# Two of block 10's four gelu groups moved from tile to tile by 48 KB transfers instead of through DRAM

## The chip, the cores and the metric

The kernel runs on one core of one Trainium2 chip. The metric is the device time of one execution in microseconds (us). TensorE (PE) does the matrix products, VectorE (DVE) and ScalarE (ACT) the elementwise work, GpSimd (POOL) and SyncE (SP) issue the DMAs; POOL also does some elementwise work. All DMAs share 16 DMA engines. SP's DMAs are queue q1 in the profile, POOL's are q0.

## What is computed

Chunked attention, then a dense layer pair with a gelu between, then a soft mixture of 8 experts with 32 slots:

```python
attn = softmax(q_c @ k_c.T / 8)            # chunks of 64 keys
x = attn @ v_c                             # 4608 tokens x 512
h = x @ w_in                               # 512 -> 2048
g = h * sigmoid(1.702 * h)
x = g @ w_out                              # 2048 -> 512
logits = x @ phi                           # 32 slots
d = softmax(logits, over tokens)
slot_input = d.T @ x                       # 32 x 512
slot_out[e] = relu(slot_input[e] @ w1[e]) @ w2[e]
out = softmax(logits, over slots) @ slot_out
```

The kernel never forms x after the gelu. It multiplies phi into w_out once, so that logits come straight from g, and it forms d.T @ g (32 x 2048) first and multiplies by w_out at the end.

## The kernel before, in words

The 4608 tokens are 12 blocks of 384. A block has 16 steps f; in each, 12 matmuls (`steps_g`) make h for 128 of the 2048 gelu channels over 384 tokens, ACT takes the tanh and DVE makes g = (tanh + 1) * h (`gelu`). h lies channels by tokens. The product d.T @ g (`dispatch`) wants g as tokens by channels, so g is transposed. Four steps make a group q (0 to 3) of 512 channels.

For blocks 1 to 10 the transposition has two parts. `store_g` has DVE transpose 32x32 squares into a slab tile g1. That leaves 32-row bands of partitions in the wrong places: what stands in band r of the partitions, position c along the row, belongs into band c, position r. After a group's fourth step, four DMAs of 192 KB write the tile to DRAM (L472). One block later `load_g` brings all four groups back (four DMAs of 768 KB, L484) into slab tiles g2, bands in their right places. `dispatch` of block b then runs (24 matmuls in the trace) in step 9 of block b+1 if that is the last block (step 12 in most others). Block 11, the last, transposes its own g on PE instead (`gemm_t`, L498), and copies it out of PSUM on DVE (L502).

After block 11 comes a tail: the last dispatch, w_out, the expert layers, whose 33.6 MB of weights are loaded in order from the end of block 9 on, nearly all by POOL (`load`, L741), and the combination.

All engines run an order written by hand: the program order of the calls is the order on each engine, and no scheduler moves anything. `block(b)` calls for each step `gemm`, then in the last block `gemm_t`, then `side(b, f)`, which starts what two tables put there, then `at`, which issues weight loads. Of these tables the parts near the change are: block 10 dispatches block 9 in step 12 and stores block 9's softmax weights ct in step 15 (`slots_b`, L647); block 11 calls `load_g(10)` in step 2, `dispatch(10)` in step 9 (the table LAST: `('g0', 2)`, `('d0', 9)`).

Two resources tie the change to the rest. The first is the pool `slab` of 11 buffers of 768 KB, which holds xh, xl, g1, g2 and later weights and outputs; a tile waits until the buffer that it gets has been read for the last time. The second is SP's queue: its DMAs are issued in program order, and each uses the next of eight semaphores, so that a DMA also waits until the one eight before it has landed.

Of the kernel before, what the change touches and what calls it, by code (L numbers as in the profile page):

```python
# [8 lines left out]
F32 = mybir.dt.float32  # L9
# [71 lines left out]
}  # L81
SIDE4 = {0: "S1", 1: "S2", 2: "S3", 3: "S4", 4: "D"}
TURN = 10
EPS = 1e-9


@with_exitstack
def attention_moe_softmoe_kernel(
# [11 lines left out]
    nc = tc.nc  # L100
# [5 lines left out]
    NB = NT // T  # L106
    NCP = T // 128
    GF = 4
# [20 lines left out]
    def slab_tile(shape, dtype, name):  # L129
        return slab.tile(shape, dtype, tag="s", name=name)  # L130
# [185 lines left out]
    def attn_e(cp, pool):  # L316
        exp(cp)
        for _ in steps_f(cp, pool):
            pass
# [5 lines left out]
    def steps_f(cp, pool):  # L325
# [3 lines left out]
        yield  # L329
        nc.vector.tensor_scalar_add(out=sm, in0=sm, scalar1=EPS)  # L330
        yield
        rs = st_p.tile([128, 2 * KD, 1], F32, tag="rs", name="rs")
        nc.vector.reciprocal(out=rs, in_=sm)  # L333
        yield
        if cp >= TURN:
            swap(cp, e, rs)
# [7 lines left out]
    def swap(cp, e, rs):  # L344
        t = et[cp] = mid_tile([128, 2 * KD, 64], "es")
        for c in range(0, 128, 64):
            for i in range(2):
                for j in range(2):
                    r, w = slice(c + 32 * i, c + 32 * i + 32), slice(c + 32 * j, c + 32 * j + 32)
                    nc.gpsimd.tensor_tensor(  # L350
                        out=t[w, :, 32 * i:32 * i + 32], in0=e[r, :, 32 * j:32 * j + 32],
                        in1=rs[r].to_broadcast([32, 2 * KD, 32]), op=ALU.mult,
                    )

    def attn_b(cp):
        if cp >= TURN:
            t = pt[cp] = ptp.tile([128, 2 * KD, 64], F32, tag="p", name="pt_sb")
            nc.vector.transpose(out=t.rearrange("p a k -> p (a k)"), in_=et.pop(cp).rearrange("p a k -> p (a k)"))
        else:
            attn_t(cp)  # L360
            attn_p(cp)
# [16 lines left out]
    def attn_x(cp, x):  # L378
        t, p = v_t.pop(cp), pt.pop(cp)
        if cp >= TURN:  # L380
            for m in (0, 2, 1, 3, 4, 6, 5, 7):
# [27 lines left out]
    def x_parts(cp, x):  # L409
# [4 lines left out]
        cs = slice(128 * i, 128 * (i + 1))  # L414
        if cp >= TURN:
            return [[y[b][:, :, cs].rearrange("p k (c q) -> p c k q", c=2) for y in (xh, xl)] + [x.rearrange("p c (k q) -> p c k q", k=KD)]]
# [14 lines left out]
    gt, g1, g2, g2t, gh = {}, {}, {}, {}, {}  # L431

    def gemm(b, f):
        for _ in steps_g(b, f):
            pass
        tanh(b, f)
        gelu(b, f)
# [22 lines left out]
    def store_g(b, f):  # L460
        t = gt[b, f]
        q, j = divmod(f, GF)
        if j == 0:
            g1[b, q] = slab_tile([128, 4, NCP, GF * 32], F32, "g1")
        nc.vector.transpose(  # L465
            out=g1[b, q][:, :, :, 32 * j:32 * (j + 1)], in_=t.rearrange("p (a b c) -> p b a c", b=4, c=32)
        )
        if j == GF - 1:
            src, d = g1.pop((b, q)), dram.tile([4, 32, 4, NCP * GF * 32], F32, tag="g", name="g_dram")
            g_dram[b, q] = d  # L470
            for fq in range(4):
                nc.sync.dma_start(  # L472
                    out=d[:, :, fq, :].rearrange("b p x -> p b x"),
                    in_=src[32 * fq:32 * fq + 32].rearrange("p b a c -> p b (a c)"),
                )


    g_dram = {}

    def load_g(b):  # L480
        g2[b] = []
        for q in range(NG):
            t = slab_tile([128, 4, NCP, GF * 32], F32, f"g2_{q}")
            nc.sync.dma_start(  # L484
                out=t.rearrange("p q a c -> p (q a c)"), in_=g_dram.pop((b, q)).rearrange("b p q x -> (b p) (q x)")
            )
            g2[b].append([t[:, :, i, :] for i in range(NCP)])
# [20 lines left out]
    def logits(b, g):  # L508
        if g == 0:
            lp[b] = ps.tile([128, T], F32, tag="lp" if b % 2 or b == 0 else "pt", name="lp")  # L510
        for j in range(4):
            f = 4 * g + j
            nc.tensor.matmul(  # L513
                out=lp[b][32 * j:32 * (j + 1), :], lhsT=wp[:, f, :], rhs=gt[b, f],
                start=(g == 0), stop=(g == NG - 1),
            )
        if g == NG - 1:
            p = lp.pop(b)
            if b == NB - 1:
                lps[b] = [mid_tile([128, T], "lps")]  # L520
                nc.scalar.activation(out=lps[b][0], in_=p, func=ACTF.Copy)
                return
            lps[b] = [
                mid_tile([128, T], f"lps{i}", F32R) if b else pro[0].tile([128, T], F32R, tag="gt", name="lps0", bufs=NF)
                for i in range(2)
            ]
            nc.scalar.activation(out=lps[b][0], in_=p, func=ACTF.Copy)
            nc.vector.tensor_tensor(out=lps[b][1], in0=p, in1=lps[b][0].bitcast(F32), op=ALU.subtract)
# [101 lines left out]
    def slots_n(b):  # L630
        lt = lg_t[b]
        cs = st_p.tile([128, NCP, 1], F32, tag="cs", name="cs")
        nc.vector.tensor_reduce(out=cs, in_=lt, axis=AX.X, op=ALU.add)
        nc.vector.tensor_scalar_add(out=cs, in0=cs, scalar1=EPS)
        nc.vector.reciprocal(out=cs, in_=cs)
# [13 lines left out]
    def dispatch(b):  # L649
        dt, cr = dt_t.pop(b)  # L650
        g = g2.pop(b)
        p = ps.tile([128, 512], F32, tag="m", name="dtg")
        for i in range(NCP):
            for j in reversed(range(4)):
                nc.tensor.matmul(  # L655
                    out=p[32 * j:32 * (j + 1)], lhsT=dt[:, i, :], rhs=g[j][i], start=(i == 0), stop=(i == NCP - 1)
                )
        if b == FIRST:
            nc.vector.tensor_copy(acc, p)
        else:  # L660
            nc.vector.scalar_tensor_tensor(out=acc, in0=acc, scalar=cr, in1=p, op0=ALU.mult, op1=ALU.add)
# [95 lines left out]
    def more_wo():  # L757
        if wo_list:
            fn, i = wo_list.pop(0)
            fn(i)  # L760
# [5 lines left out]
    def tail():  # L766
# [36 lines left out]
        nc.vector.scalar_tensor_tensor(out=s, in0=stat[b - 1][1], scalar=cr, in1=sums, op0=ALU.mult, op1=ALU.add)  # L803
        nc.vector.tensor_scalar_add(out=s, in0=s, scalar1=EPS)
        nc.vector.reciprocal(out=rs, in_=s)
# [182 lines left out]
    def side(b, f):  # L988
        for name, at in (LAST if b == NB - 1 else PLAN):
            if b == 2:  # L990
                at = {"g0": 9, "d0": 15, "b1": 5}.get(name, at)
            if b == 3:
                at = {"b3": 14}.get(name, at)
            if f != at:
                continue
            kind, i = name[0], int(name[1:])
            if kind == "l":
                if i == NG - 1:
                    logits(b - 1, i)
                else:  # L1000
                    logits(b, i)
            elif kind == "S":
                (slots_0, slots_1, slots_2, slots_3, slots_b)[i](b - 1)
            elif kind == "d":
                dispatch(b - 1)
            elif kind == "g":
                load_g(b - 1)
            elif kind == "w":
                if NPRO <= b < 10:
                    more_wo()  # L1010
            elif kind == "p":
                cp = (b + 1) * NCP + i
                pair_step(cp if cp < NB * NCP else None, cp - 2)
            elif (b + 1) * NCP + i < NB * NCP:
                cp = (b + 1) * NCP + i
                if kind == "e":
                    attn_e(cp, True)
                else:
                    attn_b(cp)
# [15 lines left out]
    def pair_step(a, c, early=False):  # L1035
        t = pair_tile("sx")
        if a is not None:
            y = attn_s(a, t[:, :, 0:256])
        if c is not None:
            z = attn_x(c, t[:, :, 256:512])  # L1040
        if early and c is not None:
            attn_y(c, z)
        if a is not None:
            attn_m(a, y)
            if a > 5:
                load_qk(a + 2)
        if c is not None:
            if not early:
                attn_y(c, z)
            if c > 5:  # L1050
                load_v(c + 2)
# [103 lines left out]
    def block(b):  # L1155
        for f in range(NF):
            gemm(b, f)
            if b == NB - 1 and f > 1:
                gemm_t(b, f - 2)
            side(b, f)  # L1160
            if b < 5:
                start((SIDE2, SIDE3, SIDE4)[b - 2].get(f, ""))
            at(f"{b}.{f}")
# [27 lines left out]
def _layouts(inputs):  # L1191
# [11 lines left out]
    v = v.reshape(n, 2, 64, -1, 2, 64)  # L1203
    v = np.concatenate([v[:TURN], v[TURN:].transpose(0, 4, 2, 3, 1, 5)])
    qk = np.concatenate([q.reshape(n, 128, -1), k.reshape(n, 128, -1)], axis=2)
# [45 lines left out]
```

## Time and profile before

| | us |
|---|---|
| median of 3 runs | 626.88 (625.63 to 627.3) |
| profiled execution | 625.93 |
| its span, first to last instruction | 624.2 |
| TensorE busy in it | 607.1 |
| DVE busy in it | 472.6 |

Block 10 runs until about 505 us of the span, block 11 from there to about 550, the tail from there to the end. A time such as 532.04 is counted from the span's start. Timeline rows merge instructions of one line that follow each other; "x4" is their number. An issue row of SP tells how long SP was busy handing the DMA over, not how long the transfer took; that is in the rows "DMA to landing".

### The profile page before, as it was taken

The page shows a single profiled execution, that of the slowest core. Times are in us where ns is not written, and L with a number is a line of the kernel's source. Part 1 is how long each engine was busy: PE and PEld are TensorE (multiplying, and loading weights), DVE is VectorE, ACT ScalarE, POOL GpSimd, SP SyncE. Part 2 cuts the span into 40 slices and gives each one's busy share as a digit, 9 for nine tenths or more (in the row PEclk, how much of TensorE's full clock was granted, in tenths as well). Part 3 has the DMA queues.
Part 4 walks back from the last instruction along what each step waited for, and adds up shares of the span by engine and source line. Part 5 has one row for each costly group of instructions (what it writes and reads, how often), then busy time and mean ns, then how long its engine had stood idle before and what let it go on. Part 6 is the DMA issues. An engine that isn't in the chain of part 4 may idle for free.

```text
span 624.2 us, 15914 instructions
## 1 busy us (share of the span) xinstructions
PE 607.1 (97%) x6542; PEld 518.4 (83%) x6542; DVE 472.6 (76%) x1005; ACT 218.3 (35%) x461; POOL 179.2 (29%) x293
## 2 busy tenths in 40 slices
PE   7999999999999999999999999999999999989993
PEld 6899888888898798998979889989989798758652
DVE  5999699789888898898888879888877746342152
ACT  4985445232232332332333332423322322121152
POOL 1010010334135134154243333342441321343320
PEclk9999999999999999999999999999999999999998
DMA  8973785559799676786695794876849879999988
GB/s 336 405 289 125 251 295 163 131 138 363 190 350 313 214 276 217 218 321 183 182 350 160 238 331 142 286 241 166 328 99 310 282 264 411 343 348 417 406 341 332
DMA packets 63992, 167.82 MB, mean 269 GB/s; under 512 B 11440, under 2 KB 33968, under 8 KB 63920
## 3 DMA queue, kind: packets, MB, share of 16 engines
q1 hardware_dynamic: 54864, 127.75, 61.8%
q0 software_dynamic: 9056, 39.06, 16.2%
q8 instruction: 51, 0.84, 0.5%
q14 instruction: 21, 0.17, 0.1%
HBM read 122.22 MB, written 44.56 MB: 267 GB/s over the span
## 4 chain that ended last, share of the span: by engine, by line
PE 85%; DVE 10%; ACT 2%; issue 1%; DMA 1%; POOL 0%; DVEq 0%; ACTq 0%; POOLq 0%
PE h L443 57%; PE lp L513 5%; PE dtg L655 5%; PE fp L896 3%; PE sx L293 3%; PE h1p L858 2%; PE op L971 2%; PE sx L385 2%; DVE gt L456 1%; DVE g L465 1%; DVE mx L309 1%; PE wpp L237 1%; PE gtp L498 1%; PE pt L370 1%; DVE e L311 1%
## 5 line engine op out<-in xcount | busy, mean ns | idle before, releaser
L443 PE MATMUL h<-xh,w 128*128 128x384 f32 x1536 | 396.1, 339 | 0.1
L443 PEld LDWEIGHTS h<-xh,w 128*128 128x128 f32 x1536 | 273.7, 188 | 25.2 <-issue 22.7
L443 PE MATMUL h<-xl,w 128*128 128x384 f32 x768 | 256.7, 335 | 0.0
L350 POOL TENSOR_TENSOR es<-e,rs 32x256 f32<-32x256 f32 x208 | 131.0, 630 | 242.9 <-DVE rs L333 200.1
L452 ACT ACTIVATE gt<-h 128x384 f32<-128x384 f32 x192 | 93.9, 490 | 218.9 <-PE h L443 218.6
L456 DVE SCALAR_TENSOR_TENSOR gt<-gt,h 128x384 f32<-128x384 f32 x192 | 103.6, 539 | 55.4 <-ACT gt L452 54.2
L443 PEld LDWEIGHTS h<-xl,w 128*128 128x128 f32 x768 | 144.1, 188 | 0.0
L465 DVE STREAM_TRANSPOSE g<-gt 128x384 f32<-128x384 f32 x176 | 100.5, 575 | 7.3 <-PE dtg L655 1.7
L741 POOL DMA_DIRECT2D w<-in_moe_w_dram x60 | 32.2, 538 | 69.4 <-PE h L443 27.6
L422 ACT ACTIVATE xh<-sx 128x512 fp32r<-128x512 f32 (+1 forms) x38 | 21.7, 578 | 75.5 <-DVE e L311 60.8
L427 DVE TENSOR_TENSOR xl<-sx,xh 128x512 fp32r<-128x512 f32 (+1 forms) x38 | 24.8, 657 | 20.0 <-ACT xh L422 20.0
L513 PE MATMUL lp<-gt,wp 128*32 128x384 f32 x384 | 39.3, 493 | 0.0
L339 POOL TENSOR_TENSOR e<-e,rs 128x512 f32<-128x512 f32 x9 | 10.0, 1110 | 101.5 <-DVE rs L333 89.6
L655 PE MATMUL dtg<-g,dt 128*32 128x512 f32 x264 | 31.1, 595 | 0.5 <-DVE gt L456 0.3
L309 DVE TENSOR_REDUCE mx<-sx 128x8 f32<-128x512 f32 (+1 forms) x37 | 23.9, 646 | 5.8 <-PE sx L293 5.8
L311 DVE TENSOR_TENSOR e<-sx,mx 128x512 f32<-128x512 f32 (+1 forms) x37 | 25.0, 675 | 1.3
L323 ACT ACTIVATE e<-e 128x512 f32<-128x512 f32 x36 | 22.6, 628 | 7.0 <-DVE e L311 6.9
L328 DVE TENSOR_REDUCE sm<-e 128x8 f32<-128x512 f32 x36 | 23.5, 652 | 0.1
L293 PEld LDWEIGHTS sx<-qk 64*64 64x64 f32 x960 | 16.7, 134 | 7.7 <-issue 7.4
L513 PEld LDWEIGHTS lp<-gt,wp 128*32 128x32 f32 x384 | 10.9, 109 | 13.1 <-issue 9.1
L156 ACT ACTIVATE stg<-stg 128x512 f32<-128x512 f32 x32 | 21.4, 676 | 0.1
L293 PE MATMUL sx<-qk 64*64 64x64 f32 x960 | 20.8, 224 | 0.0
(131 smaller groups left out, 518.4 us busy)
## 6 DMA issues: line engine op xcount, KB each, us to landing
g_dram<-g SPq DMA_DIRECT2D x176, 192.0 KB, 3.1
g<-g_dram SPq DMA_DIRECT2D x44, 768.0 KB, 7.4
qk<-in_qk_dram SPq DMA_DIRECT2D x30, 512.0 KB, 9.7
w<-in_moe_w_dram POOLq DMA_DIRECT2D x29, 512.0 KB, 8.4
w<-in_moe_w_dram POOLq DMA_DIRECT2D x16, 768.0 KB, 8.4
stg<-in_moe_w_in_dram SPq DMA_DIRECT2D x16, 512.0 KB, 6.4
stg<-in_moe_w_out_t_dram SPq DMA_DIRECT2D x16, 512.0 KB, 5.6
wo<-in_moe_w_out_dram SPq DMA_DIRECT2D x16, 512.0 KB, 3.5
```

What stands on the lines that cost most here:

```text
L293: nc.tensor.matmul(out=y[h][w, hp, :], lhsT=t[r, 0, hp, w], rhs=t[r, 1, hp, w], start=True, stop=True)
L309: nc.vector.tensor_reduce(out=mx[:, hs], in_=v, axis=AX.X, op=ALU.max)
L311: nc.vector.tensor_tensor(out=ev[:, hs], in0=v, in1=mx[:, hs].to_broadcast(list(v.shape)), op=ALU.subtract)
L350: nc.gpsimd.tensor_tensor(out=t[w, :, 32 * i:32 * i + 32], in0=e[r, :, 32 * j:32 * j + 32], in1=rs[r].to_broadcast([32, 2 * KD, 32]), op=A ...
L427: nc.vector.tensor_tensor(out=l, in0=v, in1=h.bitcast(F32), op=ALU.subtract)
L443: nc.tensor.matmul(out=h, lhsT=w_t[f][:, (0, 1, 0)[p], k, :], rhs=(xh, xh, xl)[p][b][:, k, :], start=(i == 0), stop=(i + 1 == len(steps)),)
L452: nc.scalar.activation(out=gt[b, f], in_=gh[b, f], func=ACTF.Tanh, scale=0.851)
L456: nc.vector.scalar_tensor_tensor(out=t, in0=t, scalar=1.0, in1=gh.pop((b, f)), op0=ALU.add, op1=ALU.mult)
L465: nc.vector.transpose(out=g1[b, q][:, :, :, 32 * j:32 * (j + 1)], in_=t.rearrange("p (a b c) -> p b a c", b=4, c=32))
L513: nc.tensor.matmul(out=lp[b][32 * j:32 * (j + 1), :], lhsT=wp[:, f, :], rhs=gt[b, f], start=(g == 0), stop=(g == NG - 1),)
L655: nc.tensor.matmul(out=p[32 * j:32 * (j + 1)], lhsT=dt[:, i, :], rhs=g[j][i], start=(i == 0), stop=(i == NCP - 1))
L741: eng.dma_start(out=t[:, 0:at], in_=w12[:, w_at[0]:w_at[0] + at])
```

## The change

In block 10, groups 2 and 3 are no longer written to DRAM. A function `move_g` copies g1 to g2 directly, in 16 DMAs of one 32-row band and one position each (32 rows of 1536 bytes, 48 KB). It is called after `side` in step 13 (group 2) and step 15 (group 3). `load_g(10)` then loads groups 0 and 1 alone.

```diff
+DIRECT = {2: 13, 3: 15}
...
-        if j == GF - 1:
+        if j == GF - 1 and not (b == NB - 2 and q in DIRECT):
             src, d = g1.pop((b, q)), dram.tile([4, 32, 4, NCP * GF * 32], F32, tag="g", name="g_dram")
...
+    def move_g(b, q):
+        src, t = g1.pop((b, q)), slab_tile([128, 4, NCP, GF * 32], F32, f"g2_{q}")
+        for r in range(4):
+            for c in range(4):
+                nc.sync.dma_start(out=t[32 * c:32 * c + 32, r], in_=src[32 * r:32 * r + 32, c])
+        g_moved[q] = t
...
         for q in range(NG):
+            if b == NB - 2 and q in DIRECT:
+                t = g_moved.pop(q)
+                g2[b].append([t[:, :, i, :] for i in range(NCP)])
+                continue
             t = slab_tile([128, 4, NCP, GF * 32], F32, f"g2_{q}")
...
             side(b, f)
+            for q, w in DIRECT.items():
+                if (b, f) == (NB - 2, w):
+                    move_g(b, q)
```

SP's queue before, from group 1's store in block 10 to the stores of block 10's ct in block 11 (g_dram tiles are in DRAM, g1 and g2 in slab buffers, the last number of a name only tells tiles apart):

```order
L472 DMA g_dram_6506<-g1_6361 32x4x384 x4
L472 DMA g_dram_6619<-g1_6532 32x4x384 x4
L472 DMA g_dram_6743<-g1_6645 32x4x384 x4
L647 DMA ct_dram_91<-ct_b_6753 4x32x32 x3
L484 DMA g2_0_6825<-g_dram_6340 128x1536
L484 DMA g2_1_6827<-g_dram_6506 128x1536
L484 DMA g2_2_6829<-g_dram_6619 128x1536
L484 DMA g2_3_6831<-g_dram_6743 128x1536
L647 DMA ct_dram_91<-ct_b_7018 4x32x32 x2
```

The same stretch now, where all lines of the code are 1 to 17 further down:

```order
L473 DMA g_dram_6506<-g1_6361 32x4x384 x4
L485 DMA g2_2_6698<-g1_6532 32x384 x16
L661 DMA ct_dram_91<-ct_b_6760 4x32x32 x3
L485 DMA g2_3_6765<-g1_6640 32x384 x16
L498 DMA g2_0_6849<-g_dram_6340 128x1536
L498 DMA g2_1_6851<-g_dram_6506 128x1536
L661 DMA ct_dram_91<-ct_b_7038 4x32x32 x2
```

Eight stores and two loads are gone and 32 moves have come. Group 3's transfer, which stood ahead of block 9's ct stores, now stands behind them, and the two loads that are left stand behind its 16 moves.

DVE in steps 5 to 7 of block 11 before, with the semaphores that each instruction waits for (DMAHW is one of SP's eight; the copy g_1 is the first into group 1 of block 11, in the buffer that held g1 of block 10's group 3):

```order
L456 SCALAR_TENSOR_TENSOR gt<-gt,h 128x384 [waits Activation_49]
L502 COPY g_0_6819<-gtp 128x12x32 [waits PE_49]
L538 TENSOR_REDUCE nm<-lg 128x1 [waits PE_49]
L540 TENSOR_TENSOR nm<-nm 128x1 [waits DVE_49]
L544 STREAM_TRANSPOSE lt<-lg 32x96 x4
L456 SCALAR_TENSOR_TENSOR gt<-gt,h 128x384 [waits Activation_49]
L502 COPY g_1_6946<-gtp 128x12x32 [waits DMAHW6_49,DMAHW5_49,DMAHW7_49,DMAHW4_49,PE_49]
```

The same stretch now:

```order
L457 SCALAR_TENSOR_TENSOR gt<-gt,h 128x384 [waits Activation_49]
L516 COPY g_0_6843<-gtp 128x12x32 [waits PE_49]
L552 TENSOR_REDUCE nm<-lg 128x1 [waits PE_49]
L554 TENSOR_TENSOR nm<-nm 128x1 [waits DVE_49]
L558 STREAM_TRANSPOSE lt<-lg 32x96 x4
L457 SCALAR_TENSOR_TENSOR gt<-gt,h 128x384 [waits Activation_49]
L516 COPY g_1_6966<-gtp 128x12x32 [waits DMAHW4_49,DMAHW3_49,DMAHW5_49,DMAHW2_49,DMAHW6_49,DMAHW1_49,DMAHW7_49,DMAHW0_49,PE_49]
```

The instructions stand in the same order; the copy now waits for the landing of group 3's 16 moves, over all eight semaphores, where it waited for that group's four stores. PE's instructions, too, stand in the same order in both kernels; its first matmul of `dispatch(10)` waits for the same eight semaphores where it waited for one DMA.

## Rows read from the trace of the kernel before

**Rows 1.** The page, busy time and share of the span of each engine.
```profile
PE 607.1 (97%) x6542; PEld 518.4 (83%) x6542; DVE 472.6 (76%) x1005; ACT 218.3 (35%) x461; POOL 179.2 (29%) x293
```

**Rows 2.** PE's waits, 480 to 625 us: total, times, longest, in us.
```profile
PE dtg L781 <- DVE dt L608: 1.4, 1, 1.4
PE op L971 <- ACT sr L915: 0.4, 1, 0.4
...
PE h1p L858 <- issue: 0.3, 1, 0.3
```

**Rows 3.** The chain of waits around block 11's step 9: start, length, what.
```profile
495.72 2.71 PE dtg L655 x24
498.43 0.65 PE lp L513 x8
499.08 12.71 PE h L443 x72
...
528.32 0.33 PE gtp L498 x3
...
531.72 0.33 PE gtp L498 x3
532.04 2.71 PE dtg L655 x24
534.75 0.38 PE h L443
```

**Rows 4.** SP's timeline, blocks 10 and 11: start, length in us, DMA issue.
```profile
495.53 2.12 SPq L472 DMA_DIRECT2D g_dram<-g  x4
...
507.30 2.18 SPq L472 DMA_DIRECT2D g_dram<-g  x4
509.58 2.44 SPq L647 DMA_DIRECT2D ct_dram<-ct_b  x3
512.12 2.75 SPq L484 DMA_DIRECT2D g<-g_dram  x4
```

**Rows 5.** The source lines L472 and L484, whole span: issue ns min/median/max; landing.
```profile
L472 SPq DMA_DIRECT2D g_dram<-g x176: 303/432/1797, 61.4 to 508.6; - x176
...
DMA to landing us min/median/max: 2.3/3.1/6.9
...
L484 SPq DMA_DIRECT2D g<-g_dram x44: 319/430/992, 141.2 to 514.5; - x44
...
DMA to landing us min/median/max: 5.4/7.4/10.3
```

**Rows 6.** DVE's timeline: store_g's last transpose of block 10, ct, two copies.
```profile
506.70 0.58 DVE L465 STREAM_TRANSPOSE g<-gt 128x384 f32<-128x384 f32 x1
...
508.15 0.28 DVE L642 STREAM_TRANSPOSE ct_b<-lt 128x96 f32<-128x96 f32 x1
...
524.50 0.55 DVE L502 COPY g<-gtp 128x384 f32<-128x384 f32 x1
```

**Rows 7.** POOL's timeline: the load into group 2's g1 buffer.
```profile
512.78 0.53 POOL L741 DMA_DIRECT2D w<-in_moe_w_dram  x1 [0.16 <-issue]
```

**Rows 8.** DMA queues, 515 to 530 us, then 530 to 531: packets, MB, share.
```profile
q0 software_dynamic: 761, 3.05, 51.0%
q1 hardware_dynamic: 766, 3.12, 50.8%
...
q1 hardware_dynamic: 3, 0.01, 3.0%
```

**Rows 9.** Windows: engines' busy time, clock, DMA share, GB/s.
```profile
521.00:530.00 9.00, 9.00 (x60) 8.10 (x59) 7.14 (x21) 2.83 (x8) 2.13 (x4) 1.00 1.02 417
...
535.00:550.00 15.00, 15.00 (x96) 14.00 (x95) 5.73 (x11) 2.46 (x5) 6.41 (x12) 1.00 0.93 333
...
560.00:597.00 37.00, 36.40 (x716) 25.36 (x708) 8.29 (x23) 5.69 (x16) 11.43 (x22) 1.00 0.98 393
```

**Rows 10.** DMA issues of 535 to 550 us: number, KB, median us to landing.
```profile
w<-in_moe_w_dram POOLq DMA_DIRECT2D x5, 512.0 KB, 5.3
```

More of the change, by code (lines that the diff above doesn't have):

```diff
@@ L478, in attention_moe_softmoe_kernel @@
     g_dram = {}
+    def move_g(b, q):
[4 more added lines that the diff above has]
+        g_moved[q] = t
+    g_moved = {}
     def load_g(b):
```

## The prediction

> **What bounds the kernel now.** I began with the busy shares: PE works 607.1 of 624.2 us [rows 1], so only what PE waits for, or computes, can move the time. Next PE's waits in the last 145 us, where the change lies: a 1.4 us wait for DVE in the tail, and a few of 0.3 to 0.4; none for a DMA [rows 2]. The chain of waits says the same at the one place where PE reads the data in question: dispatch(10) starts at 532.04, the moment the transposes that began at 531.72 end (0.33 us), and block 11's matmuls follow at 534.75 without a gap [rows 3]. So no work of the change lies on the path as it stands; the question is how far behind the path its transfers are, before and after.
>
> In the kernel before they are close. The four loads are issued from 512.12 on [rows 4], and the DMA engines are full (share 1.02, 417 GB/s) [rows 9], half of it with POOL's weights. Of the 3.15 MB that four loads of 768 KB make, SP's queue moves 3.12 MB from 515 to 530 us, and three packets are left after 530 [rows 8]. The data is there one to two us ahead of 532.04.
>
> **The change, part by part.**
>
> PE computes the same instructions in the same order: 0. The first matmul of dispatch waits for ten semaphores where it waited for three. No row shows what such a check costs PE; between 0 and some tenths of a us, I take 0.1.
>
> Removed from SP: two sets of four stores (2.12 and 2.18 us of issue) and two of four loads [rows 4]. Added: 32 issues. No 48 KB transfer of SP stands in the trace. The nearest are the 192 KB stores: issue 0.30 us at least, 0.43 median, 1.80 at most [rows 5]; four of them in 2.12 us with the short gaps between, 0.53 each. A move has a quarter of a store's rows, so it should be no dearer; I take 0.48 us (median plus 0.05 gap), and 0.35 to 0.53 as what is likely. The eight semaphores let eight moves be under way; with a landing of 3.1 us [rows 5] that allows one per 0.39 us, with 6.9 us one per 0.86. Now the line of due times:
>
> - Group 2's moves wait for the buffer that dispatch(9) reads last; it ends at 498.43 [rows 3]. 16 x 0.48 = 7.7, issued by 506.1, landed 3.1 later at 509.2. POOL's load into that group's g1 buffer is issued at 512.78 [rows 7]: 3.6 us in hand.
> - The ct stores behind them can go when DVE has made ct_b at 508.43 [rows 6] and take 2.44 us [rows 4]: 510.9. They hid the moves of group 2; that cover lasts while a move costs under (508.43 - 498.43) / 16 = 0.63 us.
> - Group 3's moves were free to go at 507.28 [rows 6] but now stand behind ct: 510.9 + 7.7 = 518.6, landed at 521.7. DVE's copy at 524.50 [rows 6] waits for that: 2.8 us in hand. Behind this copy wait the gelus of the next steps, and PE's transposes from 528.32 [rows 3], which need the PSUM bank it empties; the copy may therefore come 3.3 us later (528.32 - 0.55 - 524.50) before PE stops.
> - The two loads follow: 2 x 0.48, issued by 519.6. The worst landing before was 10.3, the median 7.4 [rows 5]: 527.0 to 529.9. That is 2.1 to 5.0 us ahead of 532.04, more than before, since only 1.57 MB is left to load and POOL's queue has had the engines for itself longer.
>
> The Trainium skill speaks against such pieces: "DMA: Bandwidth & Descriptors", sections Anatomy of one DMA and Rules for kernel authors, says that a transfer has a fixed cost near 2 us whatever its size, and that under 64 KB one pays mostly overhead. By its fit a move of 48 KB would take an estimated 2.1 us and a store of 192 KB 2.5. The trace agrees as far as it goes, a 192 KB store lands after 2.3 us at best [rows 5]. If the cost overlaps, the sum is unchanged.
>
> DMA traffic: 1.57 MB of stores and 1.57 MB of loads become 1.57 MB of moves. At 417 GB/s that frees 3.8 us of the DMA engines between 505 and 530. Who would use it? POOL's weights, which are needed in the tail. By 535 to 550 these land in 5.3 us [rows 10] at a share of 0.93 [rows 9], so the queue has caught up before the tail in the kernel before too, and each later load waits for a buffer that PE has to free. In the tail the engines are full again (0.98 from 560 to 597), yet PE is busy 36.40 of those 37 us [rows 9]. Worth 0; at most the 0.6 us that PE idles there, and at the bound all 3.8.
>
> DVE and ACT execute the same instructions. The slab buffers go round in another order, but each tile of weights or output again follows a tile that is read at the same step.
>
> Sum against the profiled execution: 625.93 + 0.1 = 626.0. The median of the runs is 0.95 above that execution; as medians go, I forecast 626.7, no change. A change under 0.3% (1.9 us; 625.0 to 628.8) can't be told from none here.
>
> **Rivals.**
>
> Slower: SP becomes late. If a move costs over about 0.65 to 0.7 us on SP, whether by its issue or by landing slowly while the weights fill the engines, the cover of the ct stores is gone and all 32 moves count: the loads land at 498.4 + 32d + 2.4 + 1.0 + 7.4, which reaches 532.04 at d = 0.71 (at 0.62 with a landing of 10.3). At d = 0.8 they land at 534.8, 2.8 us late: 628.8 with the profiled execution as base. At d = 1.0 they land at 541.2, 9.2 late, and group 3's moves land at 536, which stops DVE's copy earlier but in the same wait: 635. At the largest issue of any store, 1.80 plus gap, 568: 36 us. For it: the last issue of a full set is regularly the longest, and half the DMA time belongs to POOL. Against: the mean over sets of four is 0.53 to 0.55 [rows 4]. 12%, at about 632.
>
> The moves run one after another. Then each costs its landing, 3.1 us [rows 5]: 32 x 3.1 = 99 us, the loads land at 609, 77 us late: 703. Nothing in the order makes them so: a move waits for the one eight before it. 1%. This is what the rule of the fixed cost in "DMA: Bandwidth & Descriptors" of the Trainium skill would come to if it did not overlap; the four stores of a set, issued within 2.12 us while one lands after 3.1, contradict that.
>
> Faster: the loads of before end so near to 532.04 that PE waits for them in executions without a profile, or the freed 3.8 us reach the tail. The first gives up to 1 or 2 us (625.5), the second at its bound 626.9 - 3.8 = 623. For it: three packets after 530 [rows 8], 0.98 in the tail [rows 9]. Against: no wait of PE for a DMA [rows 2]. 9% that it passes 0.3%.
>
> **How the numbers follow.** No change 78%, slower by late transfers 12%, serial moves 1%, faster 9%. The no-change case alone gives 625.2 to 628.0. 8 in 10 needs little more: I leave half of the faster case below 624.8 and most of the slower above 629.5. Chances: faster 0.09, same 0.78, slower 0.13.
>
> **What would show it.** Right: dispatch(10) starts directly behind PE's transposes; SP's 16 moves take 6 to 9 us a group; the last load lands before PE arrives; DVE's first copy of group 1 in block 11 waits for no DMA; span within 1.9 us of 624.2. Wrong: a wait of PE for a DMA at dispatch(10), DVE's copy released by a DMA, moves that take over 0.65 us each on SP, or a tail in which PE's busy time per window differs.

## The result, and the profile after

| | before | changed |
|---|---|---|
| median of 9 runs each, us | 625.72 (625.63 to 627.42) | 631.6 (629.59 to 633.83) |
| profiled execution, us | 625.93 | 632.21 |
| span, us | 624.2 | 630.4 |

The ratio is 1.0081, 95% interval 1.007 to 1.0092: slower by 0.8%. I had forecast no change and given "slower" 13%.

The page of the changed kernel shows PE busy 2 us longer with the same 6542 instructions [rows 1], and the rest of the 6.2 us idle:

```profile
PE 609.1 (97%) x6542; PEld 519.9 (82%) x6542; DVE 472.6 (75%) x1005; ACT 217.7 (35%) x461; POOL 178.7 (28%) x293
```

SP's timeline (start, length in us, issues), to be held against [rows 4]:

```profile
498.05 13.44 SPq L485 DMA_DIRECT2D g<-g  x16
511.60 1.73 SPq L661 DMA_DIRECT2D ct_dram<-ct_b  x3
513.43 12.04 SPq L485 DMA_DIRECT2D g<-g  x16
525.58 0.99 SPq L498 DMA_DIRECT2D g<-g_dram  x2
```

A group of moves holds SP for 13.4 and 12.0 us, 0.84 and 0.75 per move. The ct stores go 2 us later than before and the loads 13.5 us later.

The line of the moves by itself (issue ns min/median/max, then landing), against [rows 5]:

```profile
L485 SPq DMA_DIRECT2D g<-g x32: 507/589/972, 498.1 to 524.7; - x32
...
DMA to landing us min/median/max: 3.6/5.2/8.3
```

Handing over one move costs 0.59 us, more than the median store of four times its size (0.43). The landing of 5.2 us in the last row is the median of the only four moves whose landing the row knows. In the trace each DMA brings its semaphore 16 updates, and I call a DMA landed at the last of them: so counted, the 32 moves land after 1.9 to 8.5 us, 5.8 in the median.

SP's own waits in this stretch, the moves' first; a move waits for the one eight before it:

```profile
SPq L485 <- DMA g<-g: 4.6, 3, 3.0
```

PE's waits from 480 us on, against [rows 2], first the new one:

```profile
PE gtp L512 <- DVE g L516: 3.0, 1, 3.0
PE dtg L795 <- DVE dt L622: 1.4, 1, 1.4
```

DVE's copy for which PE waits, in DVE's timeline, against the copy at 524.50 in [rows 6]:

```profile
523.63 0.55 DVE L457 SCALAR_TENSOR_TENSOR gt<-gt,h 128x384 f32<-128x384 f32 x1
530.34 0.56 DVE L516 COPY g<-gtp 128x384 f32<-128x384 f32 x1 [6.15 <-DMA g<-g_dram]
```

This is the first copy of group 1 in block 11, ready at 524.2, held up 6.15 us for the buffer of group 3's g1. The row names the loads from DRAM, but the copy's semaphores stand for the 16 moves; the last of these was issued at 524.66 and its semaphore was complete at 530.07. The two loads shared semaphores with moves and landed at 532.85 and 535.79. A releaser is inferred, and where DMAs share semaphores it can be the neighbour.

The chain of waits over the same place, against [rows 3] and a line of the kernel before, which comes first:

```profile
529.43 2.28 PE h L443 x12
```

```profile
525.58 4.76 DMA g<-g_dram
530.34 0.00 issue
530.34 0.57 DVE g L516
530.91 0.04 issue
530.95 0.90 PE gtp L512 x3
531.85 1.44 PE lp L527 x8
533.29 3.92 PE h L444 x12
537.21 0.33 PE gtp L512 x3
537.54 2.71 PE dtg L669 x24
```

The lengths tell a second thing. Three transposes take 0.90 us where they took 0.33, twelve matmuls 3.92 where they took 2.28. Windows over these stretches (engines' busy time, then granted clock, DMA share, GB/s):

```profile
525.50:531.00 5.50, 2.47 (x16) 2.15 (x14) 0.66 (x2) 0.98 (x2) 1.06 (x2) 0.91 1.01 357
531.00:533.30 2.30, 2.30 (x12) 0.73 (x12) 2.19 (x9) 0.00 (x0) 0.00 (x0) 0.50 1.02 415
533.30:537.30 4.00, 4.00 (x15) 3.97 (x15) 2.23 (x8) 0.34 (x2) 0.00 (x0) 0.56 0.28 105
537.30:541.00 3.70, 3.70 (x32) 1.50 (x30) 1.65 (x3) 0.44 (x1) 0.99 (x2) 1.00 0.45 146
```

The granted clock is 0.50 and 0.56 behind the wait, so PE runs at 1.2 GHz for most of the stretch from 531 to 537.3, and then at 2.4 again. PE had been without matmuls since 527.9.

The loss by stages, from the starts of PE's instructions in the profiled execution of each kernel, all in us. "Step 8" and dispatch(10) count from the start of dispatch(9), a point that no kernel here changes; the other columns are the length from one mark to the next.

| kernel | step 8's transposes | dispatch(10) | to the last dispatch | to the experts' first matmul | to the first sum over them | to the end |
|---|---|---|---|---|---|---|
| before | 32.51 | 36.32 | 23.35 | 8.82 | 25.13 | 34.89 |
| changed | 35.69 | 42.21 (its data was there) | 23.34 | 8.82 | 25.65 | 35.16 |
| group 2 alone | 32.51 | 38.35 | 25.28 | 8.82 | 25.14 | 34.73 |
| group 3 alone | 32.51 | 36.32 | 30.35 | 10.51 | 25.14 | 34.60 |
| weight load moved, with moves | 32.51 | 36.32 | 23.90 | 10.51 | 23.47 | 34.79 |
| weight load moved, without | 32.51 | 36.32 | 23.34 | 8.82 | 23.47 | 34.91 |
| wait filled with transposes | 35.57 | 39.38 | 23.34 | 8.82 | 25.37 | 34.76 |

The profiled execution of "group 3 alone" is the slowest of its five runs (635.25 us, median 631.09), so its row is above what that kernel usually loses.

Of the 6.3 us, 5.9 are lost before dispatch(10): 3.2 up to step 8's transposes, 2.7 behind them. The tail loses 0.8, and dispatch(9) came 0.4 earlier than before. A second wait is hidden behind the first: the last load landed 40.5 us after dispatch(9), 4.2 after the 36.3 at which dispatch(10) was due. So without the copy's wait some 4 of the 5.9 us would have been lost to the loads.

### The profile page after: what moved, and what is told of

It reads as the page before. It is cut to its first block, busy times and chain, and to the rows that moved or that the text cites. A ratio compares the mean times of both kernels' runs of the same rounds, so it can differ in the third digit from the quotient of the medians.

```text
span 630.4 us, 15949 instructions
## 1 busy us (share of the span) xinstructions
PE 609.1 (97%) x6542; PEld 519.9 (82%) x6542; DVE 472.6 (75%) x1005; ACT 217.7 (35%) x461; POOL 178.7 (28%) x293
## 4 chain that ended last, share of the span: by engine, by line
PE 89%; DVE 5%; DMA 2%; ACT 1%; issue 1%; SPq 0%; DVEq 0%; ACTq 0%
PE h L444 61%; PE lp L527 6%; PE dtg L669 5%; PE sx L294 3%; PE fp L910 2%; PE h1p L872 2%; PE sx L386 2%; PE op L985 2%; DMA stg<-in_moe_w_in_dram 1%; PE gtp L512 1%; PE wpp L238 1%; DMA g<-g_dram 1%; DVE stg L173 1%; PE pt L371 1%; PE sip L825 1%
```

## The experiments

Theory: SP is late. 16 moves hold it for 12 to 13 us where four stores held it for 2; DVE's copy waits for group 3's landing, PE for the copy, and PE then runs at half its clock. Rivals: contention costs a share per group wherever it stands; the data of dispatch(10), not the buffer, is what counts; the slow stretch has a cause of its own.

**One group alone.**

```diff
-DIRECT = {2: 13, 3: 15}
+DIRECT = {2: 13}          # and, in another kernel, {3: 15}
```

> Only group 2 moves directly; group 3 goes through DRAM as before. Theory (SP is late for group 3): the 16 moves of group 2 still hold SP from 498 to about 511.5 us, but group 3's four stores take only 2.2 us behind them, land by 518, ahead of DVE's copy at 524, and the three loads land by 530: PE waits for nothing, 625.7 to 626.5 us, as before the change. Rival (each group of moves costs its share wherever it stands, by contention of the DMA engines): half of the loss stays, about 628.7.

> Only group 3 moves directly; group 2 is stored to DRAM as before. Theory: the ct stores are not held up and are done at 511, group 3's moves then take 10 to 12 us of SP and land at 526 to 528; DVE's copy waits 2 to 3 us, which PE hardly feels (under 1 us), and the last of three loads lands at 533 to 535 against 531.7: a stall of 1 to 3 us, with some lost clock behind it, 627 to 631. Rival (each group costs half): 628.7, but with PE waiting at no single place. Rival (only the copy's buffer counts): 626 to 626.5.

Group 2 alone: 629.87 us, ratio 1.0042 (1.0007 to 1.0077). Group 3 alone: 631.09, ratio 1.0086 (1.0058 to 1.0115). The theory's expectation for group 2 was 3.4 us too low; that for group 3 was met just above the top of its range. PE's and DVE's waits in the two, first group 2 alone:

```profile
PE dtg L669 <- DMA g<-g_dram: 2.0, 1, 2.0
```

and group 3 alone:

```profile
DVE g L516 <- DMA g<-g: 2.4, 1, 2.4
...
PE dtg L669 <- DMA g<-g_dram: 3.1, 1, 3.1
```

With group 2 alone no copy waits, but SP is so late (loads issued from 517.0 instead of 512.1) that the loads miss dispatch(10) by 2.0 us, and the stage behind takes 1.9 longer. With group 3 alone the copy's 2.4 us reach PE nowhere, as I had worked out, and PE waits 3.1 for the loads within dispatch(10); wait and lost clock lengthen the stage to 30.35 us instead of 23.35. The windows behind the two waits, group 2 alone first, have a granted clock of 0.83 and 0.58:

```profile
530.00:540.00 10.00, 8.04 (x45) 5.00 (x44) 3.06 (x9) 0.49 (x1) 1.41 (x3) 0.83 0.56 217
...
535.00:542.00 7.00, 4.94 (x22) 0.97 (x22) 0.00 (x0) 0.00 (x0) 0.00 (x0) 0.58 0.36 136
```

Half the loss per group, 628.7 us, is outside group 3's interval but inside group 2's; there it is the trace that speaks against it. Each group alone makes PE wait for data at one place, and it is the second due time of the prediction. The runs of group 2 alone spread from 625.76 to 632.86, which would fit loads that come just at the edge; only one of them was traced.

**The dispatch one step later, with group 2 alone.**

```diff
-('d0', 9)
+('d0', 10)
```

> Only group 2 moves directly, and dispatch(10) comes one step (2.4 us) later, in step 10 of block 11. Theory (with group 2 alone moved, PE waits 2 us at dispatch for the last load from DRAM): the wait goes and with it the lost clock, 625.7 to 627 us. Rival (the loss of that kernel lies elsewhere): 629 to 630 as before.

626.25 us, ratio 1.0003 (0.9983 to 1.0022), as the theory has it: given 2.4 us more, the loads are there (the last landed at 534.84, dispatch(10) began at 535.07) and the median loses nothing. The kernel before with its dispatch one step later was not run, so a gain or cost of that edit by itself isn't excluded.

**Group 3's moves on GpSimd's queue.**

```diff
-                nc.sync.dma_start(
+                (nc.gpsimd if q == 3 else nc.sync).dma_start(
```

> Both groups move directly, but GpSimd's queue issues group 3's 16 moves, right when DVE's last transpose is done (507 us). Theory (SP's queue is what is late): group 3 is issued by 516 to 518 and landed by 523, SP goes on with the ct stores and the two loads at 511.5 to 514.5, which land by 524: no wait of PE for a DMA, 625.7 to 626.5 us; GpSimd's weight loads start 9 us later and catch up before the tail. Rival (contention, the moves' number): 630 to 632 as with all moves on SP.

626.59 us, ratio 1.0008 (0.9992 to 1.0024). No wait of PE for a DMA is left. SP's timeline:

```profile
498.69 12.68 SPq L485 DMA_DIRECT2D g<-g  x16
511.46 1.73 SPq L661 DMA_DIRECT2D ct_dram<-ct_b  x3
513.31 0.90 SPq L498 DMA_DIRECT2D g<-g_dram  x2
```

The same 32 moves cost nothing if group 3's do not stand ahead of the loads in one queue. So it is lateness on SP, not the moves' number. This run also takes some weight traffic away from the moves, since GpSimd's loads stand behind its own; it doesn't tell the issue's part from the traffic's.

**Another buffer for the copy.**

```diff
-    ... '11.3': 's', '11.10': 'ss',
+    ... '11.9': 's', '11.10': 'ss',
```

> All moves on SP as in the change, but one weight load goes from step 3 to step 9 of block 11, so that DVE's first copy of group 1 in block 11 gets the g1 buffer of group 2 (free by 512) instead of that of group 3 (free at 530). Theory with two waits, the copy's buffer first and the data of dispatch(10) hidden behind it: DVE's copy no longer waits, PE reaches dispatch(10) at 531.7 and now waits there for the second load, which lands at 534 to 536: a stall of 2 to 4 us and lost clock, 629.5 to 632, so little or nothing is won. Rival (the copy's buffer alone is the cause): 625.7 to 626.5.

> The kernel before with only the one weight load moved from step 3 to step 9 of block 11. If that load alone, by leaving the DMA engines to the four loads, is worth something also without the moves: 624.5 to 625.3 us. Theory (PE waits for no DMA in the kernel before): no change, 625.5 to 626.8; the repair in the run with the moves then was of the loss that the moves had made.

With the moves: 625.65 us, ratio 0.9999 (0.9973 to 1.0026). The copy no longer waits, and against my expectation dispatch(10) hardly does (24 matmuls in 3.28 us instead of 2.71): the load that was taken away, 768 KB, also left the engines to the two loads, which landed at 529.45 and 532.25. That looks like "the buffer alone". The control, the same edit without the moves, says otherwise: 624.2 us, ratio 0.9964 (0.9951 to 0.9977), below both expected ranges. The edit is a gain of its own, and it is the version that beats both kernels. With the moves part of it is lost again: 1.4 us in the medians, though three of the ten runs are at 624.2 to 624.7, as the control, and two at 631.1. In the traced execution it is 2 us. In the table they stand in the stage to the last dispatch (0.55) and the one behind it (1.7), where the granted clock is low:

```profile
555.00:561.40 6.40, 5.47 (x58) 2.98 (x62) 1.95 (x7) 1.24 (x6) 0.77 (x2) 0.73 0.93 341
```

PE waits 1.4 us at the last dispatch in every kernel here. Behind that wait the clock was low in this trace and in that of group 3 alone, and full in the others; why isn't settled.

Where the edit gains without the moves, the table shows: 1.66 us between the experts' first matmul and the first sum. The windows over the first part of it, and the matmuls with w in it, before and then with the edit:

```profile
564.20:582.60 18.40, 18.14 (x435) 15.10 (x435) 3.60 (x12) 3.05 (x9) 4.97 (x10) 1.00 1.02 414
...
L858 PE MATMUL h1p<-w,sxt x384: 269/273/403, 564.1 to 582.0; 128*32 128x128 f32 x144, 128*32 128x256 f32 x48
```

```profile
564.00:581.60 17.60, 17.60 (x386) 13.58 (x386) 3.60 (x12) 3.03 (x9) 4.40 (x9) 1.00 1.01 414
...
L858 PE MATMUL h1p<-w,sxt x336: 272/273/404, 563.9 to 581.0; 128*32 128x128 f32 x96, 128*32 128x256 f32 x72
```

At the same clock and the same DMA rate the layer takes 0.8 us less, and PE has no gap. But it is not the same program: the kernel with the edit has 48 matmuls fewer (6494 in all instead of 6542). A pair of weight units that lies in two tiles is multiplied in two narrow matmuls instead of one wide one, and moving a load of another size shifts which pairs are split. So 0.5 us of the gain are PE's work and 0.3 a gap. The other 0.9 lie up to the first sum, where the number of matmuls is the same; what made them shorter is not shown.

**The wait filled with work.**

```diff
+            if (b, f) == (NB - 1, 8):
+                p = ps.tile([128, 128], F32, tag="pt", name="spin")
+                for _ in range(28):
+                    nc.tensor.transpose(p, ident, ident)
             if b == NB - 1 and f > 1:
                 gemm_t(b, f - 2)
```

> The change, with 28 extra PE transposes (some 3.1 us at 0.11 us each, into an unused PSUM bank) ahead of the transposes in step 8 of block 11 that waited 3.0 us; nothing else differs. Theory (about half of the loss is the clock that PE loses after the wait): PE stays at its higher clock, step 8's transposes start at 531 as they did, but dispatch(10) at 534 to 535 instead of 537.5: 628.5 to 629.5 us, although PE does more work. Rival (the slow stretch has another cause, or the wait only moves): 631.6 or more.

630.35 us, ratio 1.0065 (1.0041 to 1.009). By the medians the gain over the changed kernel is 1.3 us, less than expected, and the intervals overlap, so the times alone don't show it. The profile does: step 8's transposes start as late as in the changed kernel (35.57 after dispatch(9)), but dispatch(10) 2.83 us sooner, and the clock stays up:

```profile
525.50:531.00 5.50, 5.50 (x42) 5.43 (x41) 0.63 (x2) 1.24 (x4) 1.05 (x2) 1.00 1.00 342
531.00:533.30 2.30, 2.30 (x24) 1.51 (x22) 2.22 (x8) 0.00 (x0) 0.00 (x0) 1.00 0.99 407
533.30:537.30 4.00, 4.00 (x35) 2.91 (x35) 3.26 (x10) 0.77 (x2) 0.53 (x1) 1.00 0.53 192
```

In the profiled execution, 3 us of useless work in the wait cost nothing, and dispatch(10) came 2.8 us sooner. Not all of that is the clock's: the last load landed 38.9 us after dispatch(9) here, and 40.5 in the changed kernel. There dispatch(10), at 42.2, could have come some 2 us sooner at most before it had met the loads. So the clock after the wait is shown to cost PE 2.7 us, but of the kernel's loss it holds about 2; for the rest the loads were late too.

**Fewer, larger moves.**

```diff
-        for r in range(4):
-            for c in range(4):
-                nc.sync.dma_start(out=t[32 * c:32 * c + 32, r], in_=src[32 * r:32 * r + 32, c])
+        for r in range(2):
+            for c in range(4):
+                y = slice(64 * r, 64 * r + 64)
+                nc.sync.dma_start(out=t[y, c], in_=src[y, c])
```

> The change with 8 moves of 64 rows x 1536 bytes (96 KB) a group instead of 16 of 32 rows; same bytes in all, but each half of the partitions stays where it is, so the bands are not sorted as the dispatch wants them. Theory (a move costs its issue, 0.64 us, and a wait where the one eight before it has not landed): 5 us per group and no such wait, the ct stores at 508.5 to 510.5, group 3 issued by 516, the loads by 517: no wait of PE for a DMA, 625.7 to 626.5 us. Rival (the cost goes by rows and bytes): 12 us a group as with 16 moves, 630 to 632.

This kernel leaves out the sorting of the bands. 626.2 us, ratio 1.0004 (0.9991 to 1.0017). Issue and landing of the 96 KB moves, and DVE's wait:

```profile
L486 SPq DMA_DIRECT2D g<-g x16: 502/595/1211, 498.6 to 515.8; - x16
...
DMA to landing us min/median/max: 6.6/8.7/10.8
```

```profile
DVE g L517 <- DMA g<-g: 2.0, 1, 2.0
```

The issue costs 0.6 us a DMA for 64 rows as for 32, so it does not go by rows: SP needs 5.7 and 5.1 us a group. But they land late (the row knows two of the sixteen; by their semaphores all land after 2.2 to 10.8 us, 9.7 in the median), and the copy still waits 2.0, without PE feeling it. The last load landed at 532.81, when dispatch(10) had begun at 532.14, and the stage from there takes 0.7 us longer than before. So two things make the moves late, the issue and the landing.

**The engines left to the moves.**

```diff
-    ... '10.12': 't', '10.14': 'sst', '10.15': 'v', '11.0': 'w', '11.3': 's', '11.10': 'ss',
+    ... '10.15': 'v', '11.0': 'w', '11.3': 's', '11.9': 'tsst', '11.10': 'ss',
```

> The change, with four weight loads (2.05 MB) that stood in steps 12 and 14 of block 10 put into step 9 of block 11, so that group 2's moves have the DMA engines to themselves; the slab buffers fall so that no copy of block 11 waits for a move. Theory (a move costs 0.64 us of SP; what was above that, 3 us in group 2 and 1.7 in group 3, was waiting for moves that crept behind weight packets): group 2's 16 moves take 10.2 to 10.5 us instead of 13.4, group 3's begin at 510.5 and take 10.5 to 12, the loads land by 531, PE waits for nothing in block 11. Rival (issue or the landing is slow by itself): 12.5 us or more for group 2 also without other traffic. Time 625 to 626.5 us, less if the tail's weights come better so.

> The kernel before with the same four weight loads put into step 9 of block 11, as the control for the run with the moves. Theory (without a wait in block 11 the moves are worth nothing and cost nothing): the same time as that run within 0.3%. Rival (the moves' freed 1.6 MB or their 32 issues count also without a wait): a difference above that. Where it stands against the kernel before depends on the tail's weights: 624 to 628 us.

With the moves 626.96 us, ratio 1.0022 (1.0002 to 1.0041), just above the expected range; the control 625.95, ratio 0.9992 (0.9981 to 1.0003). The moves:

```profile
L485 SPq DMA_DIRECT2D g<-g x32: 507/589/1622, 499.1 to 523.6; - x32
...
DMA to landing us min/median/max: 2.0/2.7/6.7
```

Group 2's take 11.1 us, one of them 1.6; the other 15 are 0.64 apart, which is the issue. By their semaphores they land after 1.9 to 3.8 us, ten of the sixteen within 2.0 (the row above knows four of the 32). Group 3's, beside block 11's weights, again take 12.7 and land after 3.4 to 7.1. The last load landed at 533.7, when dispatch(10) had begun at 532.6, and the stage from there takes 1.2 us longer, where I had expected no loss. The control is not slower than the kernel before, so the moves still cost about 1 us.

How traffic makes them late is seen in the queues' shares in the changed kernel while group 2's moves were being issued beside four weight loads (501 to 504.8 us; packets, MB, share), against [rows 8], where both queues carry large packets:

```profile
q0 software_dynamic: 276, 1.44, 93.3%
q1 hardware_dynamic: 80, 0.09, 6.8%
```

With packets of 4 and 6 KB on the two sides SP's queue had half of the engines. Here, with rows of 1.5 KB and three to eight moves issued and not landed, it has 6.8%: 0.09 MB in 3.8 us, 24 GB/s, where the issue alone (48 KB per 0.64 us) would allow 77. Soon after, at 504.8, SP stood for 3.0 us until the move eight before had landed. The Trainium skill, "DMA: Bandwidth & Descriptors", section Queues, rings and completion order, says that each DMA engine takes turns between its queues packet by packet, and that one of these packets can hold several descriptors. The counts fit that if a turn is an engine's share of one DMA, which is an estimate of mine: 128 rows of a load over 16 engines and one update make 9, the 32 rows of a move 3, a ratio of 3; the trace has 276 to 80, 3.5, and in [rows 8], load against load, 761 to 766. No run varied the size of the weight loads, so this is argued and not shown.

## Why the prediction was wrong, point by point

- What bounds the kernel: right that PE does, and that two due times, DVE's copy at 524.50 and dispatch(10) at 532.04, decide. Both were missed, the first with all moves, the second with one group, and in the changed kernel hidden behind the first.
- **The step that failed is the price of a move, 0.48 us.** It was "no dearer" than a store; it measured 0.84 and 0.75. Of that 0.64 is the issue and the gap (0.589 + 0.05), the same for 32 rows and 64, and most of the rest waits for the move eight before it. 16 x 0.48 = 7.7 us became 13.4 and 12.0. The reason given, a quarter of a store's rows, is what the runs contradict. [rows 4] had a nearer row for small DMAs: three ct stores, 16 KB each, took SP 2.44 us, 0.81 each.
- The issue alone would have brought the forecast to its edge and no further: with 0.64 in the prediction's line group 3 has landed by 524.5 and the loads by 529.7 to 532.6. What took it over are the waits for moves that landed late beside the weight loads.
- The landing of 3.1 us failed with it: 5.8 in the median, up to 8.5. A landing time belongs to a state of the engines: a move landed after 1.9 us with them otherwise idle and after up to 8.5 beside weight loads.
- The loads before were not "one to two us ahead of 532.04": in the kernel before the semaphore of the last load is complete at 531.41, 0.6 us ahead. And the 10.3 us of the worst landing is the worst of the ten loads, of 44, that the row knows; the four loads of block 10 took 9.8 to 16.9.
- The due times, one by one: group 2 issued by 511.5 (predicted 506.1), group 3 by 525.5 (518.6), landed at 530.1 (521.7), loads issued by 526.6 (519.6), landed at 532.9 and 535.8 (527.0 to 529.9). GpSimd's load into group 2's buffer, with 3.6 us in hand by the prediction, waited 3.5; no run shows by itself what that cost.
- The slack of the copy was right: 3.3 us until PE stops. It came 6.2 late and PE stopped for 3.0.
- The 0.1 us for the check of ten semaphores is shown by no run; in the changed kernel's chain dispatch(10) follows the transposes directly (537.21 + 0.33 = 537.54).
- The rival that came true stood at 12%: "if a move costs over about 0.65 to 0.7 us", decided at d = 0.62 to 0.71. Its loads were nearly right: with d = 0.8, the mean measured, they land at 534.8, and landed at 535.8. Its time at that d was 628.8, against 632.2 in the profiled execution. That its headline of 632 is so near the median of 631.6 is partly luck: what it lacked is the clock, 2.7 us behind a wait of 3.0, in no term of my sum.
- "If the cost overlaps, the sum is unchanged": the moves did overlap, up to eight of them, but overlap was not the limit; handing over was, and the eight semaphores.
- "No wait of PE for a DMA" was read too strictly for the tail. Another order of weight loads won 1.7 us there: a small gap put down to issue, matmuls that could be fewer, and matmuls that became shorter for a reason that stays open.
- The freed 1.57 MB was worth nothing that a run shows: with group 3's moves on GpSimd, where PE waits for no DMA, the time is that of the kernel before.

## What to carry to other kernels

Count DMAs, not bytes, where they stand in one queue ahead of something with a due time: in this kernel 16 small transfers hold the queue for 10 us by their issue alone (16 x 0.64), and held it for 12 to 13 beside a queue of large packets. When such a chain ends within a few us of its due time, price a miss with the clock: 3.0 us of idle PE were followed by 2.7 more, 2.0 with group 2 alone by 1.9. Look behind a wait for the next one: here the loads were late under the copy's wait. And run the control for every repair, and compare the page's instruction counts: one repair that seemed to take the loss away was a gain of its own, with 48 matmuls fewer.

## What was not expected of the hardware

- A 48 KB move costs SP 0.59 us to hand over, a 192 KB store in the median 0.43, a 96 KB move 0.60. GpSimd handed the same moves over in 0.50 each:

```profile
L485 POOL DMA_DIRECT2D g<-g x16: 496/498/516, 508.1 to 515.5; - x16
```

- With the engines otherwise idle most moves of SP landed after 1.9 to 2.0 us, beside weight loads after up to 8.5. "DMA: Bandwidth & Descriptors" of the Trainium skill, section Anatomy of one DMA, has a fixed cost near 2 us, fitted on GpSimd's path. The first eleven moves that GpSimd issued landed after 1.7 to 2.2 us and agree with it; SP's do too, though the section does not speak of SP's path.
- After 3.0 us without matmuls PE was granted half its clock from 530.0 to 536.8, though work was there again from 530.95. Behind the 1.4 us wait at the last dispatch it kept the full clock in most traces and lost it in two.
